# Two fp32r MLPs behind sink-window attention: the moving operand read as two interleaved streams, and fp32r rounding moved to ACT

## The chip, the cores and the metric

The kernel runs on one core of one Trainium2 chip. The metric is device time in microseconds (us) from the core's first instruction to its last, over several executions; lower is better.

## What is computed

Attention with four sink keys and a window of 128 keys, then two MLPs one after the other on the same 1536 tokens (d_model 512, d_ff 2048). All data are fp32.

```python
scores = scale * np.matmul(q, k.transpose(0, 1, 3, 2))        # 2 batches, 8 heads, 768 positions, 64 wide
a = softmax over keys that are sinks (pos < 4) or in the window (0 <= rel < 128)
x = (a @ v) as 1536 tokens x 512

def _moe_ref(x, w_in, w_out):
    h = x @ w_in
    relu6 = np.clip(h + 3.0, 0.0, 6.0)
    g = h * relu6 / 6.0
    return (g @ w_out).astype(np.float32)

def _moe2_ref(x, w_in, w_out):
    h = x @ w_in
    g = h * (1.0 / (1.0 + np.exp(-1.702 * h)))
    return (g @ w_out).astype(np.float32)
```

## The kernel before

**Precision.** The MLPs' matmuls run in fp32r. Each operand is split into two fp32r numbers: hi, the value rounded to fp32r, and lo, value minus hi. A product is three matmuls: hi·hi, hi·lo, lo·hi. Tiles with an h at the end (xyh, w0h, w1h, gh) hold the hi parts, those with an l the lo parts. hi is made by a copy that rounds (a CAST in the profile, L430 on ACT, L432 on VectorE), lo by a subtraction on VectorE (L517 for weights, L579 for g).

**Items.** The tokens are three blocks of 512, d_ff is sixteen tiles of 128. An item is one block and one tile of d_ff: `up` (L536) makes h = w_in·x for 128 rows of d_ff and 512 tokens, 4 x 3 = 12 matmuls of 512 columns into one PSUM bank; `down` (L604) multiplies g by the item's tile of w_out, again 12 matmuls of 512 columns, into four banks that are summed over the items of a block. There are 48 items for each MLP, 96 in all, and 96 x 24 = 2304 such matmuls. In between: ACT reads the bank (Relu, L548, or Sigmoid, L562) into u, VectorE completes g in u (L553 or L567), a cast makes gh, VectorE makes gl (L579). The weights of the item (w0h, w0l for up, w1h, w1l for down) are split anew for each item by `split`, from a tile wf that holds them in fp32; each of these tiles has two buffers, so a cast into one waits until TensorE has done with the item before last.

**Operands.** In up the weights stand in the array and x moves, 512 tokens in a row. In the first MLP's down w_out stands and g moves, so its result has the same layout as x and is x of the second MLP. In the second MLP's down g stands and w_out moves, so its result has tokens on partitions, and is copied and written to HBM by one DMA for every 128 tokens (L649).

**Weights.** They come as 64-bit floats through two staging tiles (stage) and are converted on the chip to fp32: one step on ACT (L448) and four on VectorE (L453, L461, L469, L476) for each of the 16 tiles of w1, and later of w2, which takes the place of w1 tile by tile while the last block of the first MLP runs and the first block of the second.

**Order.** Each engine works its queue in order, and a planner writes the queues. Each operation is given to `plan.op` with the engines that may run it and a price in ns for each, a due time, and what it reads and writes. The planner walks through time with these prices, gives a free choice to the engine that would be done first, and puts the instructions into the queues in the order so found. Items are due at a fixed step (`item_due`), stretched at the beginning where attention is worked in between. The first MLP's blocks run in five pieces (`BLOCKS`), as attention gives the tokens. Attention (scores L749, softmax L764 to L791, transposes L800, values L823 and L831, results into xyh and xyl at L430 and L850) is woven into the first 24 items.

## Time and profile before

| | us |
|---|---|
| three runs | 622.96, 623.67, 623.98 |
| median | 623.67 |
| span of the profiled execution (first to last instruction) | 622.8 |
| TensorE busy | 605.6 (97%) |
| VectorE busy | 501.1 (80%) |
| ACT busy | 261.2 (42%) |
| GpSimd busy | 1.4 (0%) |

No time beside its span is given for the profiled execution; the median lies 0.9 us above the span. A busy engine is one with at least one instruction in it; TensorE's matmuls overlap, so that it can be busy all the time and still not at its peak rate. Rows name source lines of the kernel (L536), the engine, the operation, and tiles as output<-inputs.

### The profile page before, as it was taken

The numbers are of one execution on the slowest core, as the hardware profiler recorded it, in microseconds if no ns is written. First come the engines' busy times: TensorE is split into PE (matmuls) and PEld (weight loads), VectorE is DVE, ScalarE is ACT, GpSimd is POOL, SyncE is SP. The second block draws the span as 40 slices with busy tenths as digits, with TensorE's granted clock in tenths as the row PEclk, the third lists the DMA queues.
The fourth block names the chain that finished last, engine by engine and source line by source line (L and its number), as shares of the span: only waits on it lengthen the run. The fifth ranks groups of instructions, "written<-read, shape, count | busy, mean of one in ns | idle before, by whom it ended". The sixth has DMA issues, their size and how long they took to land.

```text
span 622.8 us, 10596 instructions
## 1 busy us (share of the span) xinstructions
PE 605.6 (97%) x4242; PEld 500.4 (80%) x4242; DVE 501.1 (80%) x1061; ACT 261.2 (42%) x553; POOL 1.4 (0%) x10
## 2 busy tenths in 40 slices
PE   7889999999999999999999999999999999999996
PEld 6777887777888888888888888888888888888885
DVE  7799999899956686799999999966666666666753
ACT  5897887767546321164443554312311012211111
POOL 0000000000000000000000000000000000000000
PEclk8899999999999999999999999999999999999999
DMA  8974442554400000003343334000100000100001
GB/s 264 374 228 145 160 165 86 174 170 175 157 1 2 1 1 1 0 2 135 136 144 129 132 130 141 1 0 1 69 1 1 0 1 0 69 0 1 0 1 72
DMA packets 11175, 50.91 MB, mean 82 GB/s; under 512 B 1456, under 2 KB 1456, under 8 KB 7024
## 3 DMA queue, kind: packets, MB, share of 16 engines
q1 hardware_dynamic: 11120, 50.18, 23.6%
q8 instruction: 35, 0.57, 0.4%
q14 instruction: 20, 0.16, 0.1%
HBM read 47.02 MB, written 3.15 MB: 81 GB/s over the span
## 4 chain that ended last, share of the span: by engine, by line
PE 78%; DVE 13%; ACT 3%; DMA 3%; issue 2%; POOL 0%; ACTq 0%; SPq 0%; POOLq 0%
PE bank L536 37%; PE bank L604 36%; DMA stage<-in_w_dram 2%; DVE pexp L764 2%; DVE wf L476 2%; DVE wf L469 2%; PE bank L800 2%; PE bank L749 1%; ACT pexp L772 1%; DVE u L553 1%; PE bank L823 1%; DVE wf L453 1%; PE bank L831 1%; DVE wf L461 1%; DVE w1l L517 1%
## 5 line engine op out<-in xcount | busy, mean ns | idle before, releaser
L536 PE MATMUL bank<-xyh,w0h 128*128 128x512 f32 x384 | 151.8, 395 | 2.3 <-DVE u L553 1.5
L536 PE MATMUL bank<-xyl,w0h 128*128 128x512 f32 x384 | 149.6, 390 | 1.0 <-DVE xyl L850 1.0
L536 PE MATMUL bank<-xyh,w0l 128*128 128x512 f32 x384 | 149.7, 390 | 0.0
L562 ACT ACTIVATE u<-bank 128x512 f32<-128x512 f32 x48 | 28.7, 599 | 173.2 <-PE bank L536 173.2
L536 PEld LDWEIGHTS bank<-xyh,w0h 128*128 128x128 f32 x384 | 72.1, 188 | 17.9 <-DVE u L553 2.1
L536 PEld LDWEIGHTS bank<-xyl,w0h 128*128 128x128 f32 x384 | 72.1, 188 | 15.5 <-DVE xyl L850 1.3
L536 PEld LDWEIGHTS bank<-xyh,w0l 128*128 128x128 f32 x384 | 72.1, 188 | 15.4 <-DVE w0l L517 0.3
L604 PE MATMUL bank<-gh,w1h 128*128 128x512 f32 x192 | 76.4, 398 | 0.0
L604 PE MATMUL bank<-gh,w1l 128*128 128x512 f32 x192 | 74.9, 390 | 0.7 <-DVE w1l L517 0.7
L604 PE MATMUL bank<-gl,w1h 128*128 128x512 f32 x192 | 75.0, 390 | 0.1
L604 PE MATMUL bank<-w1h,gl 128*128 128x512 f32 x192 | 74.8, 390 | 0.0
L604 PE MATMUL bank<-w1l,gh 128*128 128x512 f32 x192 | 74.7, 389 | 0.0
L604 PE MATMUL bank<-w1h,gh 128*128 128x512 f32 x192 | 74.7, 389 | 0.0
L432 DVE CAST w0h<-wf 128x512 fp32r<-128x512 f32 x81 | 34.3, 424 | 46.4 <-PE bank L536 46.4
L517 DVE TENSOR_TENSOR w0l<-wf,w0h 128x512 fp32r<-128x512 f32 x96 | 66.2, 689 | 5.1 <-PE bank L604 0.5
L579 DVE TENSOR_TENSOR gl<-u,gh 128x512 fp32r<-128x512 f32 x96 | 66.2, 689 | 1.9
L517 DVE TENSOR_TENSOR w1l<-wf,w1h 128x512 fp32r<-128x512 f32 x96 | 66.1, 689 | 1.0
L548 ACT ACTIVATE u<-bank,three 128x512 f32<-128x512 f32 x48 | 33.0, 687 | 72.5 <-PE bank L536 72.3
L432 DVE CAST w1h<-wf 128x512 fp32r<-128x512 f32 x61 | 26.0, 426 | 33.1 <-PE bank L604 33.0
L772 ACT ACTIVATE pexp<-pexp,nb 128x196 f32<-128x196 f32 x96 | 43.2, 452 | 12.4 <-DVE nb L764 12.2
L448 ACT ACTIVATE wf<-stage 128x1024 f32<-128x1024 f32 x32 | 36.9, 1152 | 18.1 <-DMA stage<-in_w_dram 16.2
L430 ACT CAST gh<-u 128x512 fp32r<-128x512 f32 x47 | 29.2, 622 | 35.8 <-DVE u L553 19.8
(93 smaller groups left out, 834.8 us busy)
## 6 DMA issues: line engine op xcount, KB each, us to landing
stage<-in_w_dram SPq DMA_DIRECT2D x32, 1024.0 KB, 4.9
wf<-in_kq_dram SPq DMA_DIRECT2D x8, 520.0 KB, 11.1
vc<-in_vc_dram SPq DMA_DIRECT2D x12, 320.0 KB, 4.6
out_dram<-u SPq DMA_DIRECT2D x12, 256.0 KB, 2.0
vb<-in_v_dram SPq DMA_DIRECT2D x10, 256.0 KB, 6.3
kq<-in_kq_dram SPq DMA_DIRECT2D x4, 520.0 KB, 10.9
vb<-in_v_dram SPq DMA_DIRECT2D x4, 128.0 KB, 6.5
par_i<-in_params_dram SPq DMA_DIRECT2D x1, 2.0 KB, 2.9
```

Of the source, the lines that this page charges most:

```text
L430: eng.copy(out, in_)
L432: eng.tensor_copy(out, in_)
L448: lambda e: e.activation(w.tile.bitcast(F32), top.bitcast(F32), AF.Abs),
L469: lambda e: e.scalar_tensor_tensor(out=w.tile, in0=top, scalar=-0x40000000, in1=w.tile, op0=ALU.bitwise_and, op1=ALU.bitwise_or),
L476: lambda e: e.scalar_tensor_tensor(out=w.tile, in0=low, scalar=29, in1=w.tile, op0=ALU.logical_shift_right, op1=ALU.bitwise_or),
L517: lambda e: e.tensor_tensor(out=lo.tile, in0=src.tile.bitcast(F32)[:, cols], in1=hi.tile.bitcast(F32), op=ALU.subtract),
L536: e.matmul(h.tile[:, :n], w, x, start=(c == 0 and k == 0), stop=(c == NC - 1 and k == 2))
L548: lambda e: e.activation(u.tile[:, :n], h.tile[:, :n], AF.Relu, bias=three, scale=1.0),
L562: lambda e: e.activation(u.tile[:, :n], h.tile[:, :n], AF.Sigmoid, scale=1.702),
L579: lambda e: e.tensor_tensor(out=gl.tile[:, :n], in0=u.tile[:, :n], in1=gh.tile[:, :n].bitcast(F32), op=ALU.subtract),
L604: e.matmul(yb.tile, l, r, start=(begin and k == 0), stop=(end is not None and k == 2))
L772: lambda e, n=n: e.activation(pes[n].tile[:, :W], pes[n].tile[:, :W], AF.Exp, bias=nbs[n].tile, scale=-1.0, accum_out=z.tile[:, n : n + 1],),
```

## The change

Three things change.

1. A function `woven` lets a matmul read its moving operand x of 512 columns as columns 0, 256, 1, 257, 2, 258 and so on: an access pattern of 256 steps of one element, and in each 2 steps of 256 elements, which is 1024 bytes. All moving operands of up and down of both MLPs get it. The number of matmuls, columns and weight loads stays. The result's columns come out in that order, so tokens are permuted by up of the first MLP, again by its down, and again by up of the second; the DMA that writes the output puts the rows back, 16 x 8 rows of 512 in place of 128 rows in sequence. In the second MLP's down the columns of w_out would be permuted; here the host lays out w_out's columns beforehand (`apart`), so that the matmul puts them back.
2. The casts of weights and of g may no longer run on VectorE from item `second - NF + 4` on. `second` is 32 here and NF is 16, so from item 20 of 0 to 95: the fifth item of the third piece of BLOCKS (512 tokens from 512, tiles 8 to 15).
3. The planner's prices: a matmul group is planned with 2.7 ns in place of 13.3 ns beside each 512 columns, and items are due every 5184 ns in place of 5440 (5200 in the path that this run doesn't take). g's cast has the large tile's prices alone, since all items have 512 columns.

```diff
+    def woven(x):
+
+        return x.rearrange("p (a n) -> p n a", a=2)
...
         def split(i, part):
             f = items[i][3]
+            to_act = [("ACT", 520)] if i >= second - NF + 4 else [("ACT", 520), ("DVE", 335)]
...
             plan.op(
-                [("ACT", 520), ("DVE", 335)],
+                to_act,
                 lambda e: copy(e, hi.tile, src.tile.bitcast(F32)[:, cols]),
...
                         e.matmul(
-                            h.tile[:, :n], w, x, start=(c == 0 and k == 0), stop=(c == NC - 1 and k == 2)
+                            h.tile[:, :n], w, woven(x), start=(c == 0 and k == 0), stop=(c == NC - 1 and k == 2)
                         )
...
-                plan.op([("PE", 3 * (n / 2.4 + 13.3))], mm, due[i], reads=[wh, wl] + xs, writes=[h], chain="up")
+                plan.op([("PE", 3 * (n / 2.4 + 2.7))], mm, due[i], reads=[wh, wl] + xs, writes=[h], chain="up")
...
             plan.op(
-                [("ACT", 520 if big else 307), ("DVE", 335 if big else 200)],
+                [("ACT", 520)] if i >= second - NF + 4 else [("ACT", 520), ("DVE", 335)],
                 lambda e: copy(e, gh.tile[:, :n], u.tile[:, :n]),
...
-                        e.matmul(yb.tile, l, r, start=(begin and k == 0), stop=(end is not None and k == 2))
+                        e.matmul(yb.tile, l, woven(r), start=(begin and k == 0), stop=(end is not None and k == 2))
...
-                r = t0 + e4 * P
+
+                rows = out[t0 : t0 + 512, :].rearrange("(l q h) d -> q h l d", l=8, q=4)[e4]
...
-                    t += 5440 * (RATE if n < 8 else RATE2 if n < 24 else 1)
+                    t += 5184 * (RATE if n < 8 else RATE2 if n < 24 else 1)
...
+    def apart(w):
+
+        return w.reshape(-1, w.shape[1] // 2, 2).transpose(0, 2, 1).reshape(w.shape)
...
-        "w2": by_tile(x["moe2_w_in"], x["moe2_w_out"]),
+        "w2": by_tile(x["moe2_w_in"], apart(x["moe2_w_out"])),
```

The prices and the choice of engine move instructions at many places; three follow. The numbers behind the names are those of buffers; the changed kernel's lines are shifted (VectorE's subtraction for weights is L522 there, conversion's last step L480, u L558 or L572, gl L584).

VectorE while w2 is converted and the last block of the first MLP runs, from the step that ends the conversion of wf5 to the next but one gl. Before:

```order
L476 SCALAR_TENSOR_TENSOR wf5_67<-stage1_61,wf5_67 128x1024
L432 CAST w0h_3831<-wf11_73 128x512
L453 TENSOR_SCALAR wf6_68<-wf6_68 128x1024
L553 SCALAR_TENSOR_TENSOR u_3829<-u_3829,bank_3801 128x512
L517 TENSOR_TENSOR w0l_3845<-wf11_73,w0h_3831 128x512
L461 TENSOR_SCALAR wf6_68<-wf6_68 128x1024
L579 TENSOR_TENSOR gl_3856<-u_3829,gh_3847 128x512
L517 TENSOR_TENSOR w1l_3861<-wf10_72,w1h_3854 128x512
```

After:

```order
L480 SCALAR_TENSOR_TENSOR wf5_67<-stage1_61,wf5_67 128x1024
L457 TENSOR_SCALAR wf6_68<-wf6_68 128x1024
L465 TENSOR_SCALAR wf6_68<-wf6_68 128x1024
L558 SCALAR_TENSOR_TENSOR u_3833<-u_3833,bank_3805 128x512
L522 TENSOR_TENSOR w0l_3850<-wf11_73,w0h_3840 128x512
L473 SCALAR_TENSOR_TENSOR wf6_68<-stage0_60,wf6_68 128x1024
L584 TENSOR_TENSOR gl_3863<-u_3833,gh_3852 128x512
L522 TENSOR_TENSOR w1l_3868<-wf10_72,w1h_3858 128x512
```

The cast of w0h is gone from VectorE's queue, and a step of the conversion has moved up ahead of gl.

ACT at the same place, two items long. Before:

```order
L548 ACTIVATE u_3791<-bank_3760,three_126 128x512
L430 CAST w1h_3807<-wf9_71 128x512
L430 CAST gh_3812<-u_3791 128x512
L448 ACTIVATE wf6_68<-stage0_60 128x1024
L548 ACTIVATE u_3829<-bank_3801,three_126 128x512
L430 CAST gh_3847<-u_3829 128x512
L430 CAST w1h_3854<-wf10_72 128x512
```

After:

```order
L553 ACTIVATE u_3785<-bank_3758,three_126 128x512
L430 CAST w0h_3791<-wf10_72 128x512
L430 CAST gh_3802<-u_3785 128x512
L430 CAST w1h_3809<-wf9_71 128x512
L452 ACTIVATE wf6_68<-stage0_60 128x1024
L553 ACTIVATE u_3833<-bank_3805,three_126 128x512
L430 CAST w0h_3840<-wf11_73 128x512
L430 CAST gh_3852<-u_3833 128x512
L430 CAST w1h_3858<-wf10_72 128x512
```

Each item now has its cast of w0h on ACT, between the activation that reads the bank and the cast of gh. In the second MLP the same four (sigmoid, w0h, gh, w1h) make up ACT's queue.

VectorE ahead of the sixteenth gl, in the stretch where attention, the conversion of w1 and the first items share the engines. Before:

```order
L476 SCALAR_TENSOR_TENSOR wf15_77<-stage1_61,wf15_77 128x1024
L780 TENSOR_SCALAR z_2460<-z_2460 128x4
L781 RECIPROCAL z_2460<-z_2460 128x4
L791 TENSOR_SCALAR pexp_214<-pexp_214,z_2460 128x196
L791 TENSOR_SCALAR pexp_216<-pexp_216,z_2460 128x196
L432 CAST w0h_2489<-wf9_71 128x512
L517 TENSOR_TENSOR w0l_2493<-wf9_71,w0h_2489 128x512
L553 SCALAR_TENSOR_TENSOR u_2491<-u_2491,bank_2435 128x512
L517 TENSOR_TENSOR w1l_2528<-wf8_70,w1h_2521 128x512
L764 ISA pexp_218,nb_2535<-bank_2495,mask2_147 128x196
L764 ISA nb_2535 128x1
L579 TENSOR_TENSOR gl_2537<-u_2491,gh_2530 128x512
```

After:

```order
L480 SCALAR_TENSOR_TENSOR wf13_75<-stage1_61,wf13_75 128x1024
L457 TENSOR_SCALAR wf14_76<-wf14_76 128x1024
L465 TENSOR_SCALAR wf14_76<-wf14_76 128x1024
L473 SCALAR_TENSOR_TENSOR wf14_76<-stage0_60,wf14_76 128x1024
L480 SCALAR_TENSOR_TENSOR wf14_76<-stage0_60,wf14_76 128x1024
L857 TENSOR_TENSOR xyl2_93<-bank_2393,xyh2_90 128x4x128
L558 SCALAR_TENSOR_TENSOR u_2433<-u_2433,bank_2351 128x512
L522 TENSOR_TENSOR w0l_2447<-wf9_71,w0h_2440 128x512
L522 TENSOR_TENSOR w1l_2456<-wf8_70,w1h_2449 128x512
L584 TENSOR_TENSOR gl_2462<-u_2433,gh_2454 128x512
```

Before, the last conversion of w1 (wf15) and part of the next softmax stand ahead of this gl; after, the last but one (wf14) does, and the softmax has moved behind it.

## Rows read from the trace of the kernel before

**Rows 1.** The page, part 4: the chain that ended last, share by engine.

```profile
PE 78%; DVE 13%; ACT 3%; DMA 3%; issue 2%; POOL 0%; ACTq 0%; SPq 0%; POOLq 0%
```

**Rows 2.** The chain, 148 to 612 us: shares by line; a piece (start us, us, what).

```profile
by line: PE bank L536 49.0%; PE bank L604 48.2%; PE bank L800 0.8%; PE bank L749 0.7%; PE bank L823 0.7%; PE bank L831 0.6%
...
226.09 5.44 PE bank L536 x24
```

**Rows 3.** Busy us by stretches, instructions started in brackets; granted clock, DMA share, GB/s.

```profile
core 0: us, PE busy (x) PEld busy (x) DVE busy (x) ACT busy (x) POOL busy (x), PEclk, DMA share, GB/s
40.00:148.00 108.00, 103.61 (x1157) 84.17 (x1151) 105.38 (x265) 83.06 (x204) 0.00 (x0) 1.00 0.47 155
148.00:220.00 72.00, 72.00 (x621) 59.12 (x622) 52.73 (x121) 36.13 (x80) 0.00 (x0) 1.00 0.15 54
...
280.00:400.00 120.00, 120.00 (x530) 98.84 (x529) 119.01 (x182) 55.23 (x80) 0.00 (x0) 1.00 0.35 123
400.00:612.00 212.00, 212.00 (x937) 175.56 (x936) 142.40 (x261) 34.23 (x57) 0.00 (x0) 1.00 0.03 11
```

**Rows 4.** The chain, 40 to 148 us: two of its longest pieces.

```profile
94.25 6.39 DMA stage<-in_w_dram
110.72 8.07 DMA stage<-in_w_dram
```

**Rows 5.** TensorE in order of time (start us, us, what): eight transposes.

```profile
53.25 1.03 PE L800 MATMUL bank<-ident,pexp 128*128 128x128 f32 x8
```

**Rows 6.** Line L800, the transposes: duration in ns, minimum, median, maximum.

```profile
L800 PEld LDWEIGHTS bank<-ident,pexp x192: 137/140/231, 10.9 to 204.4; 128*128 128x128 f32 x192
L800 PE MATMUL bank<-ident,pexp x192: 270/273/475, 11.0 to 204.5; 128*128 128x128 f32 x192
```

**Rows 7.** Stretches, line L536 alone: TensorE busy and instructions, weight loads likewise.

```profile
148.00:612.80 464.80, 256.39 (x996) 186.04 (x996) 1.00 0.13 45
```

**Rows 8.** The same of line L604 alone.

```profile
148.00:612.80 464.80, 253.96 (x988) 185.33 (x989) 1.00 0.13 45
```

**Rows 9.** VectorE's groups, 280 to 400 us: busy us, mean ns, idle us before.

```profile
L476 DVE SCALAR_TENSOR_TENSOR wf<-stage,wf 128x1024 int32<-128x1024 int32 x16 | 19.6, 1223 | 0.1
...
L517 DVE TENSOR_TENSOR w1l<-wf,w1h 128x512 fp32r<-128x512 f32 x23 | 15.9, 690 | 0.0
...
L461 DVE TENSOR_SCALAR wf<-wf 128x1024 int32<-128x1024 int32 x15 | 10.4, 693 | 0.1
...
L432 DVE CAST w0h<-wf 128x512 fp32r<-128x512 f32 x19 | 8.0, 423 | 0.0
...
L432 DVE CAST w1h<-wf 128x512 fp32r<-128x512 f32 x7 | 3.0, 428 | 0.0
...
L432 DVE CAST gh<-u 128x512 fp32r<-128x512 f32 x3 | 1.3, 422 | 0.0
```

**Rows 10.** The whole span's groups: ACT's cast of gh, the softmax's reduction on VectorE.

```profile
L764 DVE CUSTOM_DVE_ANT_0 pexp<-bank,mask 128x196 f32<-128x196 f32 x96 | 30.6, 357 | 0.7 <-PE bank L800 0.3 <-PE bank L749 0.3
...
L430 ACT CAST gh<-u 128x512 fp32r<-128x512 f32 x47 | 29.2, 622 | 35.8 <-DVE u L553 19.8 <-DVE u L567 15.9
```

**Rows 11.** VectorE in order of time, one item of the second MLP.

```profile
494.02 0.68 DVE L567 TENSOR_TENSOR u<-bank,u 128x512 f32<-128x512 f32 x1
494.74 0.43 DVE L432 CAST gh<-u 128x512 fp32r<-128x512 f32 x1
...
495.49 0.69 DVE L579 TENSOR_TENSOR gl<-u,gh 128x512 fp32r<-128x512 f32 x1
```

**Rows 12.** TensorE in order of time: that item's first matmul with gl.

```profile
497.44 0.39 PE L604 MATMUL bank<-w1h,gl 128*128 128x512 f32 x1
```

**Rows 13.** The end of the chain: an output DMA for which ACT's copy waits.

```profile
616.12 2.19 DMA out_dram<-u
```

**Rows 14.** The page, part 6: DMA issues, KB each, us to landing.

```profile
vc<-in_vc_dram SPq DMA_DIRECT2D x12, 320.0 KB, 4.6
```

**Rows 15.** The page, part 5: the MLP's weight loads, busy us and mean ns.

```profile
L536 PEld LDWEIGHTS bank<-xyh,w0h 128*128 128x128 f32 x384 | 72.1, 188 | 17.9 <-DVE u L553 2.1
```

More of the change, by code (lines that the diff above doesn't have):

```diff
@@ L603, in mm @@
                     for k, (l, r) in enumerate(prods):
-                        e.matmul(yb.tile, l, r, start=(begin and k == 0), stop=(end is not None and k == 2))
+                        e.matmul(yb.tile, l, woven(r), start=(begin and k == 0), stop=(end is not None and k == 2))
                 plan.op(
-                    [("PE", 3 * (n / 2.4 + 13.3))], mm, due[i] + DOWN,
+                    [("PE", 3 * (n / 2.4 + 2.7))], mm, due[i] + DOWN,
                     reads=[wh, wl, gh, gl], writes=[yb], chain="down",
@@ L646, in result @@
                 )
-                r = t0 + e4 * P
+                rows = out[t0 : t0 + 512, :].rearrange("(l q h) d -> q h l d", l=8, q=4)[e4]
                 plan.op(
-                    [("SP", 262144 / RATE_DMA)], lambda e: e.dma_start(out=out[r : r + P, :], in_=o.tile), when,
+                    [("SP", 262144 / RATE_DMA)],
+                    lambda e: e.dma_start(out=rows, in_=o.tile), when,
                     reads=[o], chain="dma",
@@ L999, in general_path @@
                 plan_mlps(
-                    plan, [(s * 512, 0, NF) for s in range(NBLK)], lambda items: [5200 * n for n in range(len(items))]
+                    plan, [(s * 512, 0, NF) for s in range(NBLK)], lambda items: [5184 * n for n in range(len(items))]
                 )
```

## Prediction

> **What bounds the kernel now.** I read the chain of work that ended last first, then the busy time by stretches, then the starts of single matmuls. 78% of the chain is TensorE [rows 1]. From 148 to 612 us it is nothing else: the two MLP lines, L536 and L604, hold 97.2% of it, and its pieces are unbroken runs of their matmuls [rows 2]. In those 464 us TensorE is busy all the time [rows 3], so busy time says nothing about how well it runs; the step from one start to the next does. A run of 24 takes 5.44 us [rows 2], which is 226.7 ns for one matmul of 512 columns. The granted clock there is 1.00 [rows 3], the level of 2.4 GHz, at which 512 columns, one in a clock, take 213.3 ns. So 13.4 ns of each matmul, 32 clocks, are not columns.
>
> Before 148 us it is different: VectorE is busy 105.4 of 108 us [rows 3], the 13% of the span that the chain spends on it [rows 1] have room only here, and two waits of 6.4 and 8.1 us for weights to land lie on the chain too [rows 4]. TensorE's pace matters less there.
>
> **Term 1, the woven read.** All 2304 MLP matmuls get it; their number, columns, weights and output stay. No row of before shows a moving operand read in two streams, so its step has to be bounded. What the extra 13.4 ns are can be narrowed down: eight transposes in a row at the same clock, 128 fp32 columns each, take 1.03 us with the last one's 273 ns in it [rows 5, 6], so (1030 - 273)/7 = 108 to 109 ns a step. That is 256 clocks (106.7 ns, two a column) and some 2.4 ns. Each has a weight load of 128 columns ahead of it as the MLP's have [rows 6]. So the fixed cost of a matmul with a new weight is about 2.4 ns when the moving operand comes at half the rate, and the other 11.0 ns of the MLP's step appear where four bytes a partition are wanted in each clock. 32 clocks in 512 columns is one in 16 columns, a clock lost for every 64 bytes read from one place in sequence; alternating between two places is the kind of change that can hide such a loss. I take 213.3 + 2.4 = 215.7 ns after the change. The lower bound is 213.3 ns, a column a clock; the upper bounds are in the rivals.
>
> The Trainium skill (TensorE: Matmul & The Clock Gate, Back-to-back issue gap) gives N/2.4 + 2.5 ns for a warm matmul, 215.8 ns at 512 columns. The trace's 226.7 ns [rows 2] is 10.9 ns above it; by the page's figure as an estimate the change could give back 2304 x 10.9 = 25.1 us, and by the row alone nothing says that it can be had.
>
> What of it lies on the path: from 148 us on, 996 + 988 = 1984 matmuls [rows 7, 8], on the chain nearly without a break: 1984 x 11.0 ns = **21.8 us**. The other 320, ahead of 148 us, could give 3.5 us at most, and here the order decides. Up to the sixteenth gl VectorE does 16 conversions in before and 15 in the change, and the softmax of four heads less as well. A conversion is two steps of 1.22 us and two of 0.69 us [rows 9], the softmax has four reductions of 0.36 us [rows 10]: 3.8 + 1.4 us, some 5 us that come later, when VectorE has time (52.7 of 72 us busy from 148 to 220 us [rows 3]). Against it stand the 14.5 us in which the chain waits for weights [rows 4], which a faster TensorE doesn't shorten. I take 2.0 of the 3.5 us; bounds: -3.5 us (the planner's new order hurts by as much) to +5 us (the whole of what was moved back).
>
> **Term 2, rounding on ACT alone.** By the code this begins with item 20, the fifth of the third piece of blocks, sooner than the first MLP's last block (item 32). From there on, VectorE's casts (424 to 428 ns) become ACT casts (622 ns) [rows 9, 10]. In the order VectorE's CASTs fall from 191 to 23, ACT's rise by the same 168. After 148 us VectorE is hardly on the chain, so by itself this brings about nothing; but it is what lets term 1 stand. From 280 to 400 us, where w2 is converted, VectorE is busy 119.0 of 120 us [rows 3]: with the same work it would take the place of TensorE, which wants to do the stretch in 120 x 215.7/226.7 = 114.2 us, and 5 us of the gain would be lost. 29 casts are in that stretch, 8.0 + 3.0 + 1.3 = 12.3 us [rows 9]; without them VectorE needs some 107 us. So it stays ahead.
>
> What the casts meet on ACT: it is busy 55.2 us of these 120 and 34.2 of the next 212 [rows 3]; 29 x 0.62 = 18 us more makes 73 of 114. An item of the second MLP then costs ACT a sigmoid and three casts, four times some 0.62 us [rows 10] or 2.5 us, of 24 x 215.7 ns = 5.2 us. ACT works in order: the cast of w0h now stands between sigmoid and gh's cast, and waits for TensorE to give up w0h's buffer; behind it gh's cast waits, then VectorE's gl and the down matmuls. In before VectorE's cast of gh starts at 494.74 and gl at 495.49 us, gl ends at 496.18 [rows 11], and the first matmul that reads it starts at 497.44 [rows 12]: 1.26 us to spare. The w0h cast fits under u's 0.68 us on VectorE [rows 11], gh's cast lasts 0.2 us longer, and the 19 matmuls that the order has between an item's last up and its first down pass 0.2 us sooner: 0.4 us of the 1.26. I cost it at nothing; with the cover gone it would be 0.2 us an item, 76 items, 15 us.
>
> **The rest.** The output's rows are scattered in HBM, with the same 2 KB pieces, 256 KB and number of DMAs; only the last ones count, where one ACT copy also waits for the first DMA's landing (2.19 us, [rows 13]). Bounds: 0 and twice 2.4 us, if each landed as late as vc's 4.6 us under load [rows 14]; I take 0, since size and count of the pieces are as before. The weights are permuted on the host, which costs no device time. On SP one vb load and one stage load change places with a neighbour: nothing.
>
> **Sum.** The profiled execution's span is 622.8 us, 0.9 us under the median of 623.7. 623.7 - 21.8 - 2.0 = 599.9, say **600 us**, 3.8% less.
>
> **Rivals.**
> - *Unchanged step.* The loss could belong to the weight load rather than to the moving read: the MLP's loads last 188 ns where the transposes' last 140 ns [rows 6, 15], so the two reads may hinder each other, or the clock is lost for every 64 bytes however they come. Then only the order and term 2 are left: 623.7 us, give or take 3. Against it: the transposes load as many weight columns and pay 2.4 ns. 0.07.
> - *Half of it.* Two streams hide one loss in two: 1984 x 5.5 ns = 10.9 us, with 1 us from the early part: 612 us. 0.05.
> - *Slower.* Successive columns now lie 1 KB apart. If TensorE can't fetch from a new place in each clock, it falls to the rate at which it reads fp32, two clocks a column: 109/128 ns a column [rows 5] is 436 ns a matmul, 209 ns more, 2304 x 209 ns = 482 us, some 1105 us in all. It decides from the first MLP matmul on; even 12 clocks more a matmul (5 ns) would end at 635 us. For it: nothing in before reads so. Against it: VectorE's L476 reads every second word and takes 1223 ns for 1024 elements [rows 9], and L517, without gaps, 690 ns for 512 [rows 9], so a gap of 8 bytes costs nothing there. It is no proof for a gap of 1 KB. The Trainium skill (SBUF — State Buffer, Specifications) speaks for this rival: at least two hits on a 16-byte line are needed for full rate, and each access on a new line pays; by that rule, every column here would pay. No trace of before shows it for TensorE. 0.06.
> - *VectorE or ACT takes over* (15 us back, 615 us): inside the range's upper side by half; 0.03.
>
> **How the numbers follow.** The forecast has 0.79. Its own range: low 623.7 - 21.8 - 5 - 1 (1984 steps half a ns shorter) = 596; the bound of 213.3 ns, 4 us lower still, is left out, since the transposes keep their 2.4 ns. High 623.7 - 21.8 + 3.5 + 1.5 (a slower tail, or some waits uncovered) = 607 us. To leave out no more than 2 in 10 the range reaches on to the half gain: **596 to 613 us**, which holds most of 0.79, 0.05 and half of the last 0.03. About 0.2% is what a measurement here can tell from no change. Faster by more than that: 0.79 + 0.05 + 0.03 and 0.02 of the unchanged step, 0.89; within it 0.03; slower 0.02 + 0.06 = 0.08.
>
> **What would show it.** Right: in the stretch where both MLP lines alternate, runs of 24 take 5.18 us; L536 and L604 keep their share of the chain; VectorE falls well under full between 280 and 400 us; ACT's w0h cast takes over the wait for TensorE that VectorE's had. Wrong: runs of 24 at 5.44 us or far above; waits of TensorE for gl or gh in each item; a chain that runs over VectorE beyond 150 us by today's count; out DMAs that take longer than 2.19 us at the end.

## The result, and the profile after

The kernel before took 623.83 us in these runs (622.96 to 624.08), the changed kernel **616.88 us** (615.07 to 618.74). The ratio is 0.9896, 95% interval [0.9864, 0.9927]: faster by 1.0%, where 3.8% was forecast, and outside the range. The profiled execution of the changed kernel took 615.07 us, with a span of 613.3 us; it is the shortest of four (615.33, 618.43 and 618.74 us are the others), so an account of the two traces has to explain 622.8 - 613.3 = 9.5 us, where the medians differ by 6.9.

TensorE's step came out as forecast. A piece of the chain of work that ended last (start us, us, what), the view of [rows 2]:

```profile
225.09 5.18 PE bank L541 x24
```

24 matmuls in 5.18 us are 215.8 ns each, against 226.7 ns before. L541 and L609 are the old L536 and L604; further down, L452, L473 and L480 are the old L448, L469 and L476.

What did not come out stands in the same chain's shares by engine, the view of [rows 1]:

```profile
PE 53%; DVE 30%; ACT 6%; DMA 6%; issue 5%; POOL 0%; SPq 0%; DVEq 0%; ACTq 0%; POOLq 0%
```

TensorE's part fell from 78% to 53%, and VectorE's rose from 13% to 30%. A share of the chain says which engine the chain runs over, not how much time was lost there. The stretches, with the columns of [rows 3], say where:

```profile
core 0: us, PE busy (x) PEld busy (x) DVE busy (x) ACT busy (x) POOL busy (x), PEclk, DMA share, GB/s
40.00:148.00 108.00, 103.05 (x1059) 84.90 (x1055) 105.34 (x241) 79.16 (x179) 0.00 (x0) 1.00 0.43 142
148.00:220.00 72.00, 70.56 (x718) 58.89 (x717) 54.64 (x137) 44.88 (x110) 0.00 (x0) 1.00 0.22 72
280.00:400.00 120.00, 114.65 (x516) 95.90 (x515) 116.70 (x149) 72.21 (x105) 0.00 (x0) 1.00 0.36 123
400.00:612.00 212.00, 206.37 (x956) 180.27 (x955) 102.56 (x157) 98.07 (x169) 0.00 (x0) 0.99 0.05 16
```

Between 280 and 400 us TensorE is no longer busy throughout: 114.65 of 120 us. VectorE has lost its casts there (149 instructions instead of 182) and is still busy for 116.70 us. Its groups in this stretch show why (busy us, mean ns | idle us before); ACT's Abs of the weight stage follows behind them:

```profile
L480 DVE SCALAR_TENSOR_TENSOR wf<-stage,wf 128x1024 int32<-128x1024 int32 x16 | 24.5, 1528 | 0.1
L473 DVE SCALAR_TENSOR_TENSOR wf<-stage,wf 128x1024 int32<-128x1024 int32 x15 | 22.8, 1523 | 0.3
...
L465 DVE TENSOR_SCALAR wf<-wf 128x1024 int32<-128x1024 int32 x14 | 9.7, 690 | 0.1
```

```profile
L452 ACT ACTIVATE wf<-stage 128x1024 f32<-128x1024 f32 x14 | 21.3, 1523 | 8.6 <-DMA stage<-in_w_dram 8.4
```

VectorE's two steps that read `stage` took 1223 ns before [rows 9] and take 1523 to 1528 ns now; ACT's Abs takes 1523 ns, where its row of before, in the same stretch, was

```profile
L448 ACT ACTIVATE wf<-stage 128x1024 f32<-128x1024 f32 x14 | 16.1, 1153 | 10.3 <-DMA stage<-in_w_dram 10.2
```

These three are the operations of the MLPs that read every second 32-bit word of a buffer. Those that read neighbouring words are what they were: L465 690 ns (693 before, [rows 9]). The 31 strided steps in the stretch cost VectorE 31 x 0.30 = 9.3 us, most of the 12.3 us that the casts had freed.

TensorE's waits that the profile lists in that stretch (engine, line waited for: us in total, times, longest us) have one releaser:

```profile
PE bank L609 <- DVE gl L584: 5.3, 10, 0.9
```

One of them in order of time (start us, us, what):

```profile
312.36 1.54 DVE L473 SCALAR_TENSOR_TENSOR wf<-stage,wf 128x1024 int32<-128x1024 int32 x1
...
313.82 0.68 DVE L584 TENSOR_TENSOR gl<-u,gh 128x512 fp32r<-128x512 f32 x1
...
314.55 0.48 PE L609 MATMUL bank<-gl,w1h 128*128 128x512 f32 x1 [0.39 <-DVE gl L584]
```

gl stands behind a slowed step in VectorE's queue; gl ends at 314.50, and the matmul that wants it starts at 314.55. In before gl was ready 0.2 to 1.0 us ahead of that matmul in this stretch, with few exceptions; now it is 0.1 us for more than half of the items, which is to say that TensorE waits for it. Summing what each step of TensorE exceeds 216 ns by gives 8.9 us of waiting between 280 and 400 us (0.3 us before, against 227 ns), 7.3 us of it at matmuls that read gl. "TensorE waits" means this sum from here on; it is larger than the list's 5.3 us.

At the end there is one more loss. The first output DMA of the last block, for which ACT's fourth copy waits, took 2.19 us before [rows 13]:

```profile
605.08 3.08 DMA out_dram<-u
```

The times from the span's start at which certain items' first up matmul starts show the account. Stretches are differences of these:

| us | before | after | forecast gain | gain |
|---|---|---|---|---|
| start of item 24 | 222.5 | 221.7 | 4.8 | 0.8 |
| item 24 to 64 | 218.0 | 216.1 | 10.6 | 1.9 |
| item 64 to last matmul | 176.6 | 168.2 | 8.4 | 8.4 |
| last matmul to the end | 5.7 | 7.3 | 0 | -1.6 |

(Forecast: 2.0 us ahead of 148 us and 256 x 11.0 ns from there to item 24; then 24 x 11.0 ns an item.) The gain of the step arrives in full only where no weight is converted.

### The profile page after: what moved, and what is told of

The parts are those of the page before. It is cut to its first block, busy times and chain, and to the rows that moved or that the text cites. A ratio compares the mean times of both kernels' runs of the same rounds, so it can differ in the third digit from the quotient of the medians.

```text
span 613.3 us, 10624 instructions
## 1 busy us (share of the span) xinstructions
PE 586.0 (96%) x4242; PEld 500.3 (82%) x4242; DVE 451.3 (74%) x896; ACT 360.8 (59%) x718; POOL 1.4 (0%) x10
## 4 chain that ended last, share of the span: by engine, by line
PE 53%; DVE 30%; ACT 6%; DMA 6%; issue 5%; POOL 0%; SPq 0%; DVEq 0%; ACTq 0%; POOLq 0%
PE bank L609 24%; PE bank L541 24%; DMA stage<-in_w_dram 5%; DVE wf L480 5%; DVE wf L473 4%; DVE w1l L522 3%; DVE w0l L522 3%; DVE gl L584 3%; DVE u L558 3%; DVE wf L457 2%; ACT pexp L779 2%; ACT wf L452 2%; DVE wf L465 2%; DVE pexp L771 2%; PE bank L756 1%
## 5 line engine op out<-in xcount | busy, mean ns | idle before, releaser
L541 PE MATMUL bank<-xyh,w0h 128*128 128x512 f32 x384 | 147.1, 383 | 0.5 <-ACT xyh L430 0.5
L541 PE MATMUL bank<-xyl,w0h 128*128 128x512 f32 x384 | 145.7, 379 | 1.0 <-DVE xyl L857 1.0
L541 PE MATMUL bank<-xyh,w0l 128*128 128x512 f32 x384 | 145.7, 379 | 0.2 <-DVE w0l L522 0.2
L522 DVE TENSOR_TENSOR w1l<-wf,w1h 128x512 fp32r<-128x512 f32 x96 | 66.0, 687 | 56.9 <-ACT w1h L430 56.9
L430 ACT CAST w1h<-wf 128x512 fp32r<-128x512 f32 x90 | 55.6, 618 | 58.5 <-PE bank L609 57.7
L430 ACT CAST gh<-u 128x512 fp32r<-128x512 f32 x91 | 56.3, 619 | 44.4 <-DVE u L558 24.8
L541 PEld LDWEIGHTS bank<-xyl,w0h 128*128 128x128 f32 x384 | 72.6, 189 | 11.1 <-DVE xyl L857 1.3
L541 PEld LDWEIGHTS bank<-xyh,w0h 128*128 128x128 f32 x384 | 72.6, 189 | 10.9 <-issue 0.6
L541 PEld LDWEIGHTS bank<-xyh,w0l 128*128 128x128 f32 x384 | 72.6, 189 | 10.8 <-DVE w0l L522 0.6
L609 PE MATMUL bank<-gl,w1h 128*128 128x512 f32 x192 | 74.4, 388 | 4.0 <-DVE gl L584 3.7
L609 PE MATMUL bank<-w1h,gl 128*128 128x512 f32 x192 | 73.4, 382 | 2.0 <-DVE gl L584 1.9
L609 PE MATMUL bank<-gh,w1h 128*128 128x512 f32 x192 | 75.0, 391 | 0.2
L609 PE MATMUL bank<-w1h,gh 128*128 128x512 f32 x192 | 72.9, 380 | 0.0
L609 PE MATMUL bank<-w1l,gh 128*128 128x512 f32 x192 | 72.8, 379 | 0.0
L609 PE MATMUL bank<-gh,w1l 128*128 128x512 f32 x192 | 72.8, 379 | 0.0
L584 DVE TENSOR_TENSOR gl<-u,gh 128x512 fp32r<-128x512 f32 x96 | 66.2, 689 | 7.0 <-ACT gh L430 2.7
L572 DVE TENSOR_TENSOR u<-bank,u 128x512 f32<-128x512 f32 x48 | 32.9, 685 | 47.5 <-ACT u L567 47.5
L522 DVE TENSOR_TENSOR w0l<-wf,w0h 128x512 fp32r<-128x512 f32 x96 | 65.5, 682 | 1.7 <-ACT w0h L430 1.5
L452 ACT ACTIVATE wf<-stage 128x1024 f32<-128x1024 f32 x32 | 47.1, 1472 | 20.2 <-DMA stage<-in_w_dram 19.2
L430 ACT CAST w0h<-wf 128x512 fp32r<-128x512 f32 x84 | 51.4, 612 | 0.7 <-DVE wf L480 0.4
```

The source lines that it names most:

```text
L430: eng.copy(out, in_)
L452: lambda e: e.activation(w.tile.bitcast(F32), top.bitcast(F32), AF.Abs),
L522: lambda e: e.tensor_tensor(out=lo.tile, in0=src.tile.bitcast(F32)[:, cols], in1=hi.tile.bitcast(F32), op=ALU.subtract),
L541: e.matmul(h.tile[:, :n], w, woven(x), start=(c == 0 and k == 0), stop=(c == NC - 1 and k == 2))
L572: lambda e: e.tensor_tensor(out=u.tile[:, :n], in0=h.tile[:, :n], in1=u.tile[:, :n], op=ALU.mult),
L584: lambda e: e.tensor_tensor(out=gl.tile[:, :n], in0=u.tile[:, :n], in1=gh.tile[:, :n].bitcast(F32), op=ALU.subtract),
```

## Experiments

The theory: reading in two streams slows ACT's and VectorE's every-second-word reads of `stage`, and a slower conversion holds gl up. Rivals: it is ACT's casts or the new order of instructions; or it is the planner, whose order is made from prices of the conversion that are now too low.

### Which part of the change brings the waits

**e3_act_only**, the kernel before with ACT alone rounding from item 20 on (first the weights' cast, then g's):

```
-                [("ACT", 520), ("DVE", 335)],
+                [("ACT", 520)] if i >= second - NF + 4 else [("ACT", 520), ("DVE", 335)],
...
-                [("ACT", 520 if big else 307), ("DVE", 335 if big else 200)],
+                [("ACT", 520)] if i >= second - NF + 4 else [("ACT", 520), ("DVE", 335)],
```

> The kernel before, with one part of the change alone: from item 20 on only ACT rounds weights and g; TensorE still reads every moving operand contiguously. Theory (two-stream reads of TensorE slow the conversion's every-second-word reads of the weight stage): the step stays 226.7 ns, ACT's Abs of a weight tile stays at 1152 ns and VectorE's two strided steps at 1222 ns, TensorE waits less than 1 us in 280 to 400 us, and the time is 623.8 +- 1.5 us. Rival (it is ACT alone rounding, and the order that the planner makes of it, that delays gl): 8 to 10 us of TensorE waits appear between 280 and 400 us with the conversion at its old durations, and the time is 630 to 634 us.

Measured: 625.18 us against 624.15, ratio 1.0021 [1.0003, 1.0039]; the strided steps 1218 and 1221 ns, Abs 1152 ns; TensorE waits 1.2 us between 280 and 400 us. The rival falls: this part alone brings no slow conversion, hardly any waits, and no gain either. VectorE's groups, 280 to 400 us:

```profile
L476 DVE SCALAR_TENSOR_TENSOR wf<-stage,wf 128x1024 int32<-128x1024 int32 x16 | 19.5, 1218 | 0.2
```

**e4_weave_only**, the changed kernel with rounding free on ACT and VectorE:

```
-            to_act = [("ACT", 520)] if i >= second - NF + 4 else [("ACT", 520), ("DVE", 335)]
+            to_act = [("ACT", 520), ("DVE", 335)]
```

(and the same for g's cast)

> The changed kernel with the other part alone: two streams as in the changed kernel, but ACT or VectorE rounds, as the planner chooses, throughout. Theory (contention): Abs stays near 1470 ns and the strided VectorE steps near 1470 ns in the stretch with woven matmuls; VectorE takes some 20 to 29 roundings of about 420 ns back, so TensorE waits at least the 8.9 us of the changed kernel between 280 and 400 us and up to 20 us: 617 to 628 us. Rival (ACT alone is the cause): the waits vanish and the time is 605 to 609 us.

Measured: 616.0 us (614.36 to 616.55), ratio 0.9861 [0.9826, 0.9896]; Abs 1622 ns, the strided steps 1496 and 1525 ns between 280 and 400 us; TensorE waits 8.3 us. One of VectorE's groups, one of ACT's, and the stretch:

```profile
L473 DVE SCALAR_TENSOR_TENSOR wf<-stage,wf 128x1024 int32<-128x1024 int32 x13 | 19.8, 1525 | 0.1
```

```profile
L452 ACT ACTIVATE wf<-stage 128x1024 f32<-128x1024 f32 x13 | 21.1, 1622 | 8.3 <-DMA stage<-in_w_dram 8.3
```

```profile
280.00:400.00 120.00, 116.69 (x519) 95.88 (x518) 118.92 (x172) 58.14 (x76) 0.00 (x0) 1.00 0.34 118
```

The slow conversion and the waits come with the two streams. The theory's number was too high: 616.0 against 616.88 us, with ranges that overlap, so ACT's part is worth nothing measurable beside the slowed conversion.

**e5_late**, two streams from item 64 on only, when all weights are converted:

```
-                            h.tile[:, :n], w, woven(x), ...
+                            h.tile[:, :n], w, woven(x) if i >= len(items) - 2 * NF else x, ...
```

(likewise for the down matmul, the planner's price of a group, the due times, the first block's output copy and the other blocks' output rows)

> The changed kernel, but reading two streams only from item 64 on, when no weight tile is converted any more; the planner's price of a TensorE group follows. Theory (contention): conversion at 1152 and 1222 ns as before, TensorE waits under 1 us in 280 to 400 us, and only the last 32 items gain: 32 x 24 x 11.0 ns = 8.4 us, less 0 to 1.6 us at the end: 615.4 to 617.5 us, the same as the changed kernel with a third fewer two-stream items. Rival (a cause that has nothing to do with the streams, such as ACT's share or the new order): the waits of 8.9 us stay, and the time is 624 to 626 us.

Measured: 617.15 us (615.75 to 618.16), conversion at 1154 and 1219 to 1222 ns, waits 1.2 us. VectorE's group:

```profile
L480 DVE SCALAR_TENSOR_TENSOR wf<-stage,wf 128x1024 int32<-128x1024 int32 x16 | 19.5, 1219 | 0.2
```

The time equals that of the changed kernel, which reads two streams three times as long: there, most of what 64 items could gain from the step is lost again.

### How far apart the streams are

These kernels differ from the changed one by the distance between the two streams; the columns are read in groups of twice n, and the output tiles go to neighbouring rows. The lines are those of e11_d64; the others have n = 32, 16 or 4 in place of 64, and e14_4x16 has a=4, n=16:

```
-        return x.rearrange("p (a n) -> p n a", a=2)
+        return x.rearrange("p (b a n) -> p b n a", a=2, n=64)
...
-                rows = out[t0 : t0 + 512, :].rearrange("(l q h) d -> q h l d", l=8, q=4)[e4]
+                rows = out[t0 + e4 * P : t0 + (e4 + 1) * P, :]
```

The host's layout of w_out follows. With n of 16, 32 and 64 the rows are not put back, so the output's rows stand in another order than the reference's. On TensorE, VectorE and ACT the MLPs' instructions stand in the same order as in the changed kernel, for n from 4 to 64.

> The changed kernel with the two streams 64 bytes apart (in groups of 32 columns, 16 and 16) instead of 1 KB; output tiles go to neighbouring rows, so that their order is not the reference's. Theory 1 (any second stream hides what a contiguous read loses once in 16 columns): step 215.8 ns, strided conversion steps near 1470 ns, time 614 to 617 us. Theory 2 (two streams this near to each other ask for the lines no earlier than one stream): step 226.7 ns or more, conversion at 1152 and 1222 ns, no TensorE waits, about 622 to 625 us. A step of 215.8 ns with the conversion at its old durations would be the best of both, at 605 to 607 us.

> As the run with 64 bytes, with the streams 256 bytes apart (groups of 128 columns, 64 and 64). By theory 1 the same step of 215.8 ns and the same conversion near 1470 ns as at 1 KB, 614 to 617 us; a conversion that is slowed less than at 1 KB would say that the distance of the streams decides, and would give 607 to 613 us.

> The changed kernel with two streams 128 bytes apart, in groups of 64 columns (32 and 32); output tiles go to neighbouring rows, so that their order is not the reference's. It lies between the 64 bytes that left the conversion alone (600.7 us) and the 256 bytes that slowed it as 1 KB does (615.3 us). If contention begins beyond neighbouring lines of 64 bytes, the conversion takes 1460 to 1530 ns and the time is 614 to 617 us; if it begins beyond 128 bytes, 1152 and 1222 ns and 600 to 602 us.

> The changed kernel with the two streams 16 bytes apart, in groups of 8 columns (4 and 4). Three such readings in a row put a token back in its place, so the output needs no scattered rows. With streams 64 bytes apart the step was 215.84 ns and the strided conversion steps kept 1220 ns; at 256 bytes and 1 KB they took 1460 to 1530 ns. If what counts is that the second stream lies within the next 64 bytes or nearer: step 215.8 ns, no slowed conversion, 599 to 602 us. If each 64 bytes of a contiguous operand cost one clock because two neighbouring pieces are asked for one after the other, streams 16 bytes apart change nothing of that: step 226.7 ns, 622 to 625 us.

| run | distance | us (range) | ratio | step ns | Abs, strided steps ns, 280-400 us |
|---|---|---|---|---|---|
| after | 1 KB | 616.88 (615.07-618.74) | 0.9896 | 215.85 | 1523; 1523, 1528 |
| e11_d64 | 256 B | 615.28 (614.38-617.57) | 0.9869 [0.9843, 0.9894] | 215.84 | 1540; 1531, 1525 |
| e15_d32 | 128 B | 601.18 (600.30-603.49) | 0.9641 [0.9608, 0.9674] | 215.83 | 1187; 1222, 1223 |
| e10_d16 | 64 B | 600.73 (599.98-604.06) | 0.9638 [0.9604, 0.9672] | 215.83 | 1175; 1222, 1219 |
| e13_d4 | 16 B | 599.38 (599.01-600.21) | 0.9602 [0.9578, 0.9626] | 215.83 | 1153; 1222, 1220 |

This is the cleanest separation that the runs hold. The step is the same at every distance. From 128 to 256 bytes the conversion jumps from about its old durations to the slow ones, and the time by 14 us. Neither numbered theory of e10_d16 came: the step is fast and the conversion keeps its durations, the third case named there, some 5 us faster than its 605 to 607 us. e11_d64 came as theory 1 had it, e15_d32 as its second case and e13_d4 as its first. Between 280 and 400 us, in order: a group of VectorE's and TensorE's waits in e11_d64; then a group of VectorE's, one of ACT's and the stretch in e13_d4:

```profile
L480 DVE SCALAR_TENSOR_TENSOR wf<-stage,wf 128x1024 int32<-128x1024 int32 x16 | 24.4, 1525 | 0.1
```

```profile
PE bank L609 <- DVE gl L584: 5.1, 10, 0.9
```

```profile
L480 DVE SCALAR_TENSOR_TENSOR wf<-stage,wf 128x1024 int32<-128x1024 int32 x15 | 18.3, 1220 | 0.1
```

```profile
L452 ACT ACTIVATE wf<-stage 128x1024 f32<-128x1024 f32 x14 | 16.1, 1153 | 5.3 <-DMA stage<-in_w_dram 5.3
```

```profile
280.00:400.00 120.00, 120.00 (x557) 104.82 (x556) 109.44 (x154) 71.10 (x110) 0.00 (x0) 1.00 0.33 114
```

At 16 bytes TensorE is busy throughout again, it waits 0.2 us, and VectorE's 109.4 us are near the 107 of the forecast. So is the time: 599.4 us against 600. In the expectation of e13_d4 the second idea fell: the contiguous read's loss is gone even where both streams lie within 32 bytes, so two neighbouring 64-byte pieces asked for one after the other don't explain it. And e13_d4 needs no scattered rows, since three such readings put each token back in its place.

**e14_4x16**, four streams 64 bytes apart:

> The changed kernel with four streams 64 bytes apart, in groups of 64 columns (4 times 16). Three such readings too put a token back in its place; output rows are neighbours. If the stretch that the streams cover decides the contention (64 bytes harmless, 256 bytes not): step 215.8 ns with conversion slowed in part, 603 to 616 us. If only the distance from one stream to the next decides: conversion at 1152 and 1222 ns, no TensorE waits in 280 to 400 us, 599 to 602 us.

Measured: 716.38 us, ratio 1.1487 [1.1453, 1.1520]. Neither expectation's time held, since the step itself is slower; the conversion's durations are the second's. Single matmuls in order of time (start us, us, what), 0.27 us apart, 268.9 ns on average:

```profile
450.10 0.43 PE L541 MATMUL bank<-xyh,w0h 128*128 128x512 f32 x1
450.37 0.43 PE L541 MATMUL bank<-xyl,w0h 128*128 128x512 f32 x1
450.64 0.43 PE L541 MATMUL bank<-xyh,w0l 128*128 128x512 f32 x1
```

The conversion stays at 1165, 1222 and 1220 ns although the four streams span 256 bytes, so the span alone is not what slows it; but TensorE itself runs slower here, and the two can't be separated in this run.

### Which reads collide

**e19_up_only**, the changed kernel with two streams 1 KB apart in up matmuls alone:

```
-                        e.matmul(yb.tile, l, woven(r), ...
+                        e.matmul(yb.tile, l, r, ...
```

(with the price of a down group, the due times, the weights' layout and the output rows to match)

> The changed kernel with two streams 1 KB apart for the up matmuls (x operand) only; down matmuls read g and weights contiguously, priced so. The up step is 215.8 ns, the down step 226.7. If any two-stream read 1 KB apart collides with the conversion: Abs and the strided steps near the middle, 1300 to 1400 ns on average, TensorE waits of 2 to 6 us between 280 and 400 us, 615 to 621 us. If only the down operand (g and weight tiles) collides: 1152 and 1222 ns, no waits, 613 to 615 us. If only the up operand collides: the slowed durations are as long as in the changed kernel (1630 ns at worst) whenever an up group runs, and the same middle on average, so the durations are to be split by what TensorE runs beside them.

Measured: 618.98 us, ratio 0.9924 [0.9904, 0.9944]; Abs 1241 ns and the strided steps 1317 and 1303 ns, means over all 32 conversions; waits 4.7 us. A single conversion shows it best. In order of time, one strided step beside up matmuls and one beside down matmuls:

```profile
355.46 1.53 DVE L473 SCALAR_TENSOR_TENSOR wf<-stage,wf 128x1024 int32<-128x1024 int32 x1
...
356.01 0.38 PE L541 MATMUL bank<-xyh,w0l 128*128 128x512 f32 x1
```

```profile
361.56 1.22 DVE L480 SCALAR_TENSOR_TENSOR wf<-stage,wf 128x1024 int32<-128x1024 int32 x1
...
361.99 0.39 PE L609 MATMUL bank<-w1h,gl 128*128 128x512 f32 x1
```

Sorting all conversions by what ran on TensorE for over nine tenths of their time:

| mean ns (count) | beside up | beside down | beside neither |
|---|---|---|---|
| after, Abs | 1590 (3) | 1602 (4) | 1169 (3) |
| after, L473 | 1541 (4) | 1513 (6) | 1217 (4) |
| e19_up_only, Abs | 1597 (2) | 1141 (10) | 1167 (3) |
| e19_up_only, L473 | 1531 (6) | 1221 (6) | 1221 (5) |

Either operand slows the conversion when it is read in two streams, and a contiguous read doesn't. The expectation that the x operand or the weight operand might be special falls; what counts is the pattern. The theory's means of 1300 to 1400 ns missed Abs, which happened to stand mostly beside down matmuls.

### How much of it is the order

**e7_price**, the changed kernel with nothing but two prices of the planner altered, that of Abs and that of each of the two strided steps (one of them shown):

```
-            [("ACT", 1036)],
+            [("ACT", 1480)],
...
-            [("DVE", 1135)],
+            [("DVE", 1390)],
```

> The changed kernel with the planner told the new prices of the conversion: 1480 for Abs on ACT (1036), 1390 for VectorE's two strided steps (1135). Theory 1 (contention makes VectorE the bound between 280 and 360 us, where it is busy over 97%): no order recovers more than a part, the waits there stay at 5 to 9 us, time 613 to 617 us. Rival (the work would fit, only the order made from prices that are too low puts gl late): waits fall under 2 us, time 606 to 610 us. In either case the conversion's durations stay near 1470 ns.

Measured: 600.27 us (599.42 to 601.25), ratio 0.9621 [0.9587, 0.9654]. The rival's mechanism holds, and theory 1 fell by 13 us: the conversion is as slow as ever and VectorE as full, but TensorE hardly waits (0.9 us). The time is 6 us below the rival's 606 us as well. Against the trace of the changed kernel 8.0 us come back between items 24 and 64, and another 7.6 us ahead of item 24 (which starts at 214.1 instead of 221.7 us), where the expectation had nothing. A group of VectorE's, and the stretch:

```profile
L473 DVE SCALAR_TENSOR_TENSOR wf<-stage,wf 128x1024 int32<-128x1024 int32 x14 | 21.4, 1530 | 0.1
```

```profile
280.00:400.00 120.00, 119.86 (x554) 103.87 (x553) 116.30 (x153) 77.22 (x112) 0.00 (x0) 1.00 0.32 114
```

So 116 of 120 us on VectorE is no limit in itself, and the order matters. One visible difference is what stands ahead of gl. VectorE in order of time in the changed kernel, and then in e7_price:

```profile
318.38 0.68 DVE L522 TENSOR_TENSOR w0l<-wf,w0h 128x512 fp32r<-128x512 f32 x1
318.98 1.51 DVE L473 SCALAR_TENSOR_TENSOR wf<-stage,wf 128x1024 int32<-128x1024 int32 x1
320.41 0.68 DVE L584 TENSOR_TENSOR gl<-u,gh 128x512 fp32r<-128x512 f32 x1
```

```profile
318.38 0.68 DVE L522 TENSOR_TENSOR w0l<-wf,w0h 128x512 fp32r<-128x512 f32 x1
318.98 0.68 DVE L457 TENSOR_SCALAR wf<-wf 128x1024 f32<-128x1024 f32 x1
319.58 0.68 DVE L584 TENSOR_TENSOR gl<-u,gh 128x512 fp32r<-128x512 f32 x1
```

In the changed kernel a strided step stands directly ahead of gl 10 times out of 22 between 280 and 400 us; in e7_price 6 times out of 23. It also spends a lead that nobody needed: w0l was ready 3.6 to 6 us ahead of its matmul for 20 of the 22 items from 34 to 55 in the changed kernel, and in e7_price 8 of them had no more than 2.1 us. That the order decides is shown, since only prices were altered; which feature of it does so is not. In e4_weave_only a strided step stands directly ahead of gl only 4 times out of 22, as often as in the kernel before, and TensorE still waits 8.3 us, with VectorE busy 118.92 of 120 us.

**e16_before_price**, the kernel before with these two prices:

> The kernel before with nothing but the planner's new prices of the conversion (Abs 1480 for 1036, the two strided VectorE steps 1390 for 1135), without two streams. In the changed kernel these prices alone gave 16.6 us. If they do so by fitting the order to a conversion that the streams slow down, the kernel before has nothing to win from them: TensorE waited 0.3 us between 280 and 400 us, so 622 to 626 us. If the order that they make is better whatever the streams (it also put less TensorE waiting ahead of 280 us: 16.0 us against 21.1), the kernel before gains too: 612 to 619 us.

Measured: 620.43 us (619.78 to 622.61), ratio 0.9948 [0.9923, 0.9972], between the two expectations. It gains 3.4 us, all of it ahead of item 24, which starts at 218.4 instead of 222.5 us. So a part of what the prices gave the changed kernel ahead of item 24 has nothing to do with the slowed conversion.

**e17_d4_price**, streams 16 bytes apart and these prices:

> Streams 16 bytes apart as in the run of that name (599.4 us, conversion at 1152 and 1222 ns) and the planner's prices of the run with new prices (1480 and 1390). If distance and prices return the same microseconds, only what the prices gave the kernel before (3.4 us, all ahead of item 24) can come on top: 596 to 597 us. If the new order is worth nothing or costs where the conversion is not slowed: 599 to 602 us. If both gains added in full: 583 us, which TensorE's own time forbids (2304 matmuls at 215.8 ns and the attention).

Measured: 597.13 us (595.96 to 597.56), ratio 0.9567 [0.9548, 0.9587]. Prices gave the changed kernel 16.6 us and the kernel with near streams 2.3 us: distance and order return for the most part the same microseconds. Item by item it is 4.4 us up to item 24 (216.7 to 212.3 us), 0.2 us lost from there to item 64, and 1.6 us lost after the last matmul.

### The end

**e8_rows**, the changed kernel with output tiles in neighbouring rows (only the line with `rows`, as above; the output's rows stand in another order here too):

> The changed kernel, but each output tile is written to 128 neighbouring rows, as before, so that the rows of the output stand in another order than the reference's. Theory (scattered rows cost at the end): output DMAs land after 2.0 us instead of 2.9, ACT's fourth copy of the last block waits 0.96 us instead of 1.91, the stretch from the last matmul's start to the end is 5.7 us instead of 7.3, and the time falls by 1.6 us, to 615.3. Rival (the end is longer for another reason): the end stays at 7.3 us.

**e9_aside**, with the output tiles in buffers that the first MLP leaves free:

```
-                o = Buf(cls="u")
+                o = Buf(cls="aside")
```

> The changed kernel, with the output tiles of the second MLP in the four buffers 'aside' that the first MLP leaves free, instead of the three buffers u. Theory (the end hangs on the fourth copy, which waits for the first output DMA to free a u): the fourth copy waits for nothing but its bank, the end is shorter by 1.9 to 2.9 us although the DMAs still take 2.9 us, and the time is 614.0 to 615.0 us. Rival (the last DMA's own landing sets the end, or DMAs that now run together slow each other): gain under 0.8 us.

Measured: e8_rows 615.87 us (612.96 to 616.20), from the last matmul's start to the end 6.15 us instead of 7.28; e9_aside 614.82 us (614.54 to 617.35), 6.19 us. The chain's end in e8_rows, and in e9_aside:

```profile
606.85 2.39 DMA out_dram<-u
```

```profile
601.58 5.26 PE bank L609 x24
606.84 0.02 issue
606.86 0.58 ACT aside L430
```

Each takes about 1.1 us from the end, by its own way: a shorter landing, or no wait for one. e8_rows was expected at 5.7 us, and e9_aside's gain lies between theory (1.9 us or more) and rival (under 0.8). In the times themselves it can't be told from the spread of the runs. The page's output DMAs (KB each, median us to landing) in the changed kernel, and in e8_rows:

```profile
out_dram<-u SPq DMA_DIRECT2D x12, 256.0 KB, 2.9
```

```profile
out_dram<-u SPq DMA_DIRECT2D x12, 256.0 KB, 2.0
```

**e18_d4_price_aside**, the last two put together with near streams:

> As the run with streams 16 bytes apart and new prices, and output tiles of the second MLP in the four free buffers 'aside'. In the changed kernel that shortened the stretch from the last matmul's start to the end from 7.28 to 6.19 us, where the output DMA took 2.9 us; with neighbouring rows it is 5.97 us and the fourth copy's wait is 0.96 us at most. So 0.4 to 1.0 us less than without: the end at 5.0 to 5.6 us, the time 595 to 597 us if the prices add, 598 to 601 us if they do not.

Measured: 596.23 us (595.59 to 597.48), ratio 0.9560 [0.9538, 0.9583], the fastest median of these runs and as expected, 27.7 us under the kernel before. Its end was 7.0 us, longer than the 5.0 to 5.6 expected, and against e17_d4_price the buffers' part can't be told from the spread.

## Why the prediction was wrong

**Bound now, and term 1: right.** The bound (from 148 us on), the step (215.7 forecast, 215.8 ns measured) and the place of its loss in the moving read were right; the Trainium skill's figure (TensorE: Matmul & The Clock Gate, Back-to-back issue gap), 215.8 ns at 512 columns, is met to the tenth of a ns with two streams. Where nothing hinders it, from item 64 on, the gain is the forecast 8.4 us. The picture of a clock lost for every 64 bytes is not borne out: it divides all 32 clocks by the columns, the fixed 2.4 ns among them, while two streams return 226.7 - 215.8 = 10.9 ns, or 26 clocks, one in 20 columns. Why a contiguous read loses them stays open.

**Term 2: the step that failed.** The prediction took VectorE's work between 280 and 400 us, subtracted 12.3 us of casts, and concluded "So it stays ahead". It counted the conversion's strided steps at the durations of [rows 9], which were measured beside contiguous reads of TensorE. Beside two streams 1 KB apart they take 1.52 us, so 9.3 us came back. It also took gl's spare time, 1.26 us, from an item of the second MLP [rows 11, 12], where no weights are converted; in before it is 0.2 to 1.0 us between 280 and 400 us. Two conditions together made 8.9 us of waiting of it, and of the 21.8 us of term 1 the part from item 24 to 64 came out at 1.9 instead of 10.6 us: the slowdown, and an order that leaves gl late when it comes. With either of them gone (e13_d4, e7_price) the time is 599 to 600 us, which is the forecast. In e13_d4 it is so stretch by stretch: 5.8 us gained up to item 24, 10.6 us from there to item 64, 8.4 us behind it, and 0.3 us lost at the end. In e7_price it is partly luck: 8.4 us come ahead of item 24, against 4.8 forecast, and make up for 2.0 us lost at the end. Whether ACT has to do the rounding once the streams are near was not tried; alone it gained nothing (e3_act_only).

**The early part: mis-sized.** By item 24 0.8 us were gained instead of 4.8. With near streams it is 5.8 us (item 24 at 216.7 us) in the same order of instructions, so the term's idea was right, and 5.0 us of it went to the same slowdown: the first MLP's weights are converted there, the strided steps ahead of item 24 took VectorE 45.3 us instead of the 39.0 us with near streams, and VectorE is busy for 105.3 of the 108 us up to 148 us.

**The end: costed at 0, measured 1.6 us**, inside the bounds of 0 to 4.8 us. Scattered rows alone brought the landing from 2.0 to 2.9 us in the median of the page, although pieces and sizes are the same; that reason for 0 was wrong.

**The rivals.** "VectorE or ACT takes over", with 15 us back and 615 us, named the time that came, and VectorE did come onto the path; but its 15 us were worked out for another mechanism, ACT's cast of w0h ahead of gh's, so that the number is luck. e4_weave_only lets VectorE round again and takes 616.0 us. "Slower" looked at the gap between columns only as a cost to TensorE. There it cost nothing, and the rule cited with it (the Trainium skill, SBUF — State Buffer, Specifications: two hits on a 16-byte line, or each access pays) does not show here as the rival took it, column by column: successive columns share no such line at 64 bytes to 1 KB, and a matmul takes 215.8 ns. Each line is still come back to for all four of its columns, so these runs don't say what fewer hits would cost. The cost fell on ACT's and VectorE's reads, and no rival had that.

That other engines' reads would slow down could not be read from before: no row there shows a two-stream read. What could be read was that the gain of 280 to 400 us hung on the durations of three operations, and on gl's spare time of about 1 us or less; a range that let these durations move by a quarter would have been some 9 us wider.

## What to carry to other kernels

An access pattern that makes one engine faster can make others slower, so compare the mean durations of every unchanged operation before looking for new waits. When an operation's duration changes, a planner's prices have to follow, since an order made from old ones can turn a slowdown that there is room for into waiting (here two prices returned 16.6 us with the operations as slow as before; the same prices gave the kernel before 3.4 us, so not all of it is that). Where several patterns have the same speed, try one with a short distance too: here 16 bytes did for TensorE what 1 KB did, and left the other engines alone.

## What the runs showed of the hardware

- A moving fp32r operand of 512 columns takes 226.7 ns a matmul when read contiguously and 215.8 ns when read as two streams in turn, at any distance tried from 16 bytes to 1 KB. Four streams 64 bytes apart take 268.9 ns, 53 ns or 127 clocks of 2.4 GHz more than two, about one clock in four columns.
- While TensorE reads two streams 256 bytes or 1 KB apart, ACT's and VectorE's reads of every second 32-bit word slow down: Abs from 1.15 to about 1.6 us, the VectorE steps from 1.22 to about 1.52 us, for the time that they lie beside such matmuls. At 128 bytes and less Abs is at most 3% longer (1187 ns at 128 bytes, 1175 at 64, 1153 at 16) and the VectorE steps keep their 1.22 us. VectorE's steps that read neighbouring words (L457, L465) take 683 to 706 ns between 280 and 400 us in all these runs, 690 and 693 ns in before: no slowdown like that of the others.
- The Trainium skill (Trainium Architecture — The Big Picture, What this means for kernel authors) says that on SBUF's engine side only VectorE and GpSimd contend. These traces differ: TensorE's reading pattern lengthens these reads of ACT's by a third and of VectorE's by a quarter, with GpSimd busy for 1.4 us in the whole span. The measurement decides.
- Why the boundary lies between 128 and 256 bytes, what the engines hinder each other at, and whether reads with other gaps than one word are hit, wasn't tried and stays open.
